# Block means of the values: from accumulating loads to twelve matmuls, with a new order of work

## The chip, the cores and the metric

The kernel runs on one core of a Trainium2 chip. The metric is the device time of one execution in microseconds (us); lower is better. Besides it there is a profile of one execution, taken by the hardware profiler.

## What is computed

Local and global attention over 2 batches, 8 heads, 768 positions of 64 values, followed by two feed-forward layers over the 1536 tokens of 512 values. The values' block means are what the change is about: `v_sum`, the mean over each block of 32 positions, 24 blocks per batch.

```python
k_sum = k.reshape(B, H, nb, 32, D).max(axis=3)
v_sum = v.reshape(B, H, nb, 32, D).mean(axis=3)
scores_l = scale * q @ k^T, kept where |i - j| < 16, else -1e9
scores_s = scale * q @ k_sum^T + log(32)
a = softmax(concat(scores_l, scores_s))
x = a @ concat(v, v_sum)                    # (1536, 512)
h = x @ w_in;  x = (h * sigmoid(1.702 h)) @ w_out
h = x @ w_in2; x = (h * cos(h)) @ w_out2
```

## The kernel before

**Tiling.** The attention goes by units of 128 queries, of which there are 12 (6 per batch). A unit scores its queries against a window of 96 keys per half unit and the 24 block maxima of its batch, so each row of scores has 120 columns; it then transposes the probabilities on TensorE and multiplies them with a values tile whose first 96 rows are the window and whose last 24 rows are the block means. The feed-forward layers go by three token tiles of 512 (four units each), and in each by 16 pieces of 128 hidden values: `h` matmuls (L697), the activation on ScalarE and VectorE, `out` matmuls (L793) that add into four PSUM banks. Weights and activations are each split into a high and a low part, and three products of them are added.

**The start.** The first four units ("early") are worked in two halves of four heads each, so there are eight groups of early scores ("early s", L406), of masking on VectorE (L413), of exponentials on ScalarE (L420), of transposes ("early t", L455), of copies out of PSUM (L465) and of value products ("early pv", L435). Their values tiles are `vw` and the three `vy`. The first weights (`raw` tiles, 1 MB each, L604) are loaded and split beside this (L616 scaling on ScalarE, L622 and L626 on VectorE, then L643 high part and L647 low part). Units 4 to 11 ("main") are put between the matmuls of the first layer's token tiles and use PSUM banks `a0` and `a1` for scores (L406), transposes (L521) and products.

**The block means before.** The rows of a batch's values are loaded so that several rows of one block come to the same partition: a first load writes a tile (L312, SP's queue), and further loads, issued by GpSimd, add to it during the transfer (`accum_op=ALU.add`, L317). Batch 0 has three tiles of 128 partitions with one accumulating load each. Batch 1 has one tile of 96 partitions with seven accumulating loads, each of which waits for the one before. A matmul with a constant selection matrix `blk` (L380, `vsum_mm`) adds what is left over partitions and scales: three matmuls for batch 0 in an "h" bank (`vsum0`), one for batch 1 in bank `a0` (`vsum1`, created at step 2 of the feed-forward loop, L961). ScalarE and GpSimd copy batch 0's means into the values tiles (`put_vsum`, L352); ScalarE copies batch 1's into `vsb` (L963), from where they go into `vw` before unit 6.

**The order of work.** Nothing is ordered by the place in the source alone. Every step is an `Op` with an engine, an estimated duration and what it depends on; `Ring` objects add the dependences of reused buffers. `order_of` (L177) runs a list scheduler over the steps with a priority per kind (the path length to the end plus `BONUS`), models TensorE's two clock levels with `PE_COLUMNS`, and the steps are then emitted in the order of their planned starts. Each engine takes its instructions in that order. The chain `wanted` (L926) fixes the order of SP's first loads: keys of the first half, queries, mask, identity, `blk`, the three tiles of batch 0's values, keys and queries of the second half, the window values of unit 0, the first weights, the other window values, the second weights. Batch 1's values and keys come behind that (L935).

Of the kernel before, what the change touches and what calls it, by code (L numbers as in the profile page):

```python
# [10 lines left out]
FP32 = mybir.dt.float32  # L11
# [3 lines left out]
ALU = mybir.AluOpType  # L15
# [4 lines left out]
DM, DFF = 512, 2048  # L20
# [32 lines left out]
PE_COLUMNS = {"s": 1920, "early s": 960, "t": 960, "pv": 1800, "early pv": 900, "vsum": 1920, "vsum1": 1440}  # L53
PE_DEFAULT = 3 * U
BONUS = {
    "add vf": -3414.5, "add vf1": -18784.9, "added vf": -13944.7, "added vf1": 6958.2, "at": 11219.4,
    "early at": 4634.7, "early exp": -16393.5, "early load v": -13487.3, "early load w": 3402.3,
    "early norm": -7393.4, "early pv": -21291.9, "early s": -1812.0, "early sum": -5913.0, "early t": 11259.2,
    "early ttr": -13278.6, "early w hi": -9898.3, "early w join": 1295.3, "early w lo": -17457.0,
    "early w low": 8007.6, "early w scale": -8113.8, "early xc": -3323.6, "early xl": -3755.5, "evac": 13034.7,  # L60
    "exp": 3944.6, "g hi": -14757.5, "g lo": -32277.0, "gate": 6833.5, "h": 1746.4, "ksum": -9033.2,
    "load blk": -15626.5, "load ident": -10094.2, "load k": 32.4, "load k1": -5996.2, "load kf0": 11676.2,
    "load kf1": -9957.5, "load mask": 17224.8, "load q": 5269.3, "load qf0": -25960.1, "load qf1": 9488.3,
    "load v": 509.5, "load vf": 17019.9, "load vf1": -16213.9, "load w": -6084.3, "norm": 18693.0, "out": 1747.8,
    "put ksum": 7597.4, "put vsum": -13657.5, "put vsum pool": 517.6, "pv": -5659.2, "s": -293.9, "store": -8775.6,
    "sum": -7343.5, "t": 22163.2, "ttr": -7908.6, "vsb": 368.0, "vsum": 4596.7, "vsum1": -11612.0, "w hi": -3717.9,
    "w join": -5696.0, "w lo": 4131.9, "w low": 4594.6, "w scale": -6735.7, "x hi": -18171.4, "x lo": -12909.2,
    "xc": -5390.2,
# [142 lines left out]
def local_global_attention_two_ffn(  # L211
# [56 lines left out]
    vf = [[w_p.tile([n, DM], FP32, name="vf", tag="w1") for _ in range(a)] for n, a in ((128, 3), (GW, 1))]  # L268
# [8 lines left out]
    blk = ex[1][:, 1536:1792]  # L277
    ksum = ex[1][:, 1792:1984].rearrange("p (b h n) -> p b h n", b=B, h=H // 2)
# [28 lines left out]
    s_vf = [[], []]  # L307
    for b in range(B):
        n = (2, 8)[b]
        r = v[b].rearrange("(t p r) d -> t p r d", p=vf[b][0].shape[0], r=n)  # L310
        for a, t in enumerate(vf[b]):
            o = ring["w1"].take(dma(("load vf", "load vf1")[b], (0.9, 0.7)[b], t, r[a, :, 0, :]), True)  # L312
            d_vf[b].append(o)
            for k in range(1, n):
                go = op(
                    ("add vf", "add vf1")[b], "POOL", 1.1,
                    lambda t=t, i=r[a, :, k, :]: nc.gpsimd.dma_start(out=t, in_=i, accum_op=ALU.add), o  # L317
                )
                o = op(("added vf", "added vf1")[b], "DMA", (0.9, 0.7)[b], lambda: None, go)
                for x in (go, o):  # L320
                    ring["w1"].use(x)
            s_vf[b].append(o)
# [50 lines left out]
    def vsum_mm(b, tag, parts):  # L373
        ps, mm = {}, None
        for a, (sel, t, n, dep) in enumerate(parts):
# [10 lines left out]
            ring["w1"].use_of(n, dep)  # L386
# [3 lines left out]
    def vsum0(tag):  # L390
        return vsum_mm(0, tag, [(blk[:, 16 - 8 * a:16 - 8 * a + GC], vf[0][a], a, s_vf[0][a]) for a in range(3)])

    def vsum1(tag):
        return vsum_mm(1, tag, [(blk[0:GW, 136:136 + GC], vf[1][0], 3, s_vf[1][0])])
# [457 lines left out]
    for a in range(1, UT):  # L852
        ring["w1"].use_of(3 + a, d_v[a])
# [197 lines left out]
```

## Time and profile before

| | |
|---|---|
| median of 3 runs | 600.13 us (599.36 to 601.23) |
| the profiled execution | 600.15 us, of which 598.4 us are its span |
| TensorE (PE) busy | 582.9 us, 97% |
| its weight loads (PEld) | 473.7 us, 79% |
| VectorE (DVE) busy | 396.5 us, 66% |
| ScalarE (ACT) busy | 294.4 us, 49% |
| GpSimd (POOL) busy | 13.1 us, 2% |
| mean granted clock of TensorE | 0.981 |
| DMA | 55.07 MB; plain queue 52.36 MB, accumulating queue 2.16 MB |

The span is what lies between the first and the last instruction. An engine's busy time is an average over stages that have different limits, so the table says only which engine can be the bound as a whole; where it waits, and for whom, is read from the views of single stretches below. A matmul in 32-bit floats leaves two records, so "x2" of the block means (L380) is one matmul. Records of successive matmuls overlap: what one costs in a row of them is read from the distance of starts. A row of the view by stretch holds the stretch, its length, the busy time (and number of instructions) of PE, PEld, DVE, ACT and POOL in this order, the granted clock of TensorE as a share of 2.4 GHz, the busy share of the DMA engines and what they moved in GB/s.

### The profile page before, as it was taken

The numbers are of one execution on the slowest core, as the hardware profiler recorded it, in microseconds if no ns is written. First come the engines' busy times: TensorE is split into PE (matmuls) and PEld (weight loads), VectorE is DVE, ScalarE is ACT, GpSimd is POOL, SyncE is SP. The second block draws the span as 40 slices with busy tenths as digits, with TensorE's granted clock in tenths as the row PEclk, the third lists the DMA queues.
The fourth block names the chain that finished last, engine by engine and source line by source line (L and its number), as shares of the span: only waits on it lengthen the run. The fifth ranks groups of instructions, "written<-read, shape, count | busy, mean of one in ns | idle before, by whom it ended". The sixth has DMA issues, their size and how long they took to land.

```text
span 598.4 us, 8609 instructions
## 1 busy us (share of the span) xinstructions
PE 582.9 (97%) x3310; PEld 473.7 (79%) x3310; DVE 396.5 (66%) x810; ACT 294.4 (49%) x607; POOL 13.1 (2%) x21
## 2 busy tenths in 40 slices
PE   6999998999999999999999999999999999999996
PEld 4578886888888888888888888888888888888885
DVE  5789897856322244778779866667666667765663
ACT  4788666856212454756657633234433344433332
POOL 2011110000000000000000000000000000000000
PEclk8699998999999999999999999999999999999999
DMA  8969897652000130545550000000100000100001
GB/s 297 300 223 292 262 268 231 200 154 72 1 0 1 44 97 28 212 146 206 211 174 38 1 1 0 1 1 0 72 0 2 0 1 0 71 1 1 0 1 71
DMA packets 24281, 55.07 MB, mean 92 GB/s; under 512 B 9904, under 2 KB 14384, under 8 KB 20144
## 3 DMA queue, kind: packets, MB, share of 16 engines
q1 hardware_dynamic: 23024, 52.36, 26.1%
q0 software_dynamic: 1216, 2.16, 2.2%
q8 instruction: 26, 0.43, 0.3%
q14 instruction: 15, 0.12, 0.1%
HBM read 51.37 MB, written 3.15 MB: 91 GB/s over the span
## 4 chain that ended last, share of the span: by engine, by line
PE 88%; DMA 7%; ACT 2%; DVE 1%; issue 1%; SPq 0%; POOL 0%; ACTq 0%
PE h_ps L697 41%; PE acc L793 41%; DMA vf<-in_v_dram 4%; DMA raw<-in_w_dram 4%; PE x_ps L435 2%; PE s_ps L406 1%; PE t_ps L521 1%; DVE wc L626 1%; ACT wc L616 1%; PE vs_ps L380 1%; SPq L261 0%; DVE w L647 0%; PE t_ps L455 0%; ACT ex L420 0%; DVE raw L622 0%
## 5 line engine op out<-in xcount | busy, mean ns | idle before, releaser
L697 PE MATMUL h_ps<-xh,w 128*128 128x512 f32 x1152 | 302.8, 392 | 0.0
L793 PE MATMUL acc<-g,w 128*128 128x512 f32 x1152 | 300.9, 390 | 0.0
L697 PEld LDWEIGHTS h_ps<-xh,w 128*128 128x128 f32 x1152 | 215.4, 188 | 46.3 <-issue 1.7
L793 PEld LDWEIGHTS acc<-g,w 128*128 128x128 f32 x1152 | 215.7, 188 | 45.4 <-issue 0.6
L753 ACT CAST g<-gt 128x512 fp32r<-128x512 f32 x96 | 59.7, 622 | 138.3 <-PE acc L793 132.2
L757 DVE TENSOR_TENSOR g<-gt,g 128x512 fp32r<-128x512 f32 x96 | 66.1, 689 | 88.3 <-ACT g L753 88.1
L745 ACT ACTIVATE gt<-gt,half_pi 128x512 f32<-128x512 f32 x48 | 34.7, 723 | 64.2 <-DVE gt L741 64.0
L749 DVE TENSOR_TENSOR gt<-gt,h_ps 128x512 f32<-128x512 f32 x48 | 33.0, 688 | 25.5 <-ACT gt L745 25.5
L647 DVE TENSOR_TENSOR w<-wc,w 128x512 fp32r<-128x512 f32 x64 | 43.5, 686 | 1.0 <-ACT w L643 0.7
L721 ACT ACTIVATE gt<-h_ps 128x512 f32<-128x512 f32 x48 | 28.6, 597 | 30.2 <-PE h_ps L697 28.6
L643 ACT CAST w<-wc 128x512 fp32r<-128x512 f32 x64 | 38.5, 617 | 7.9 <-DVE wc L626 7.9
L626 DVE SCALAR_TENSOR_TENSOR wc<-wc,raw 128x1024 uint32<-128x1024 uint32 x32 | 39.2, 1224 | 3.1 <-ACT wc L616 1.9
L616 ACT ACTIVATE wc<-raw 128x1024 f32<-128x1024 f32 x32 | 37.0, 1156 | 7.3 <-DMA raw<-in_w_dram 7.2
L729 DVE TENSOR_SCALAR gt<-gt 128x512 f32<-128x512 f32 x48 | 20.5, 427 | 24.6 <-ACT gt L721 24.2
L725 DVE SCALAR_TENSOR_TENSOR gt<-gt,h_ps 128x512 f32<-128x512 f32 x48 | 32.8, 683 | 3.4 <-ACT gt L719 3.0
L733 DVE SCALAR_TENSOR_TENSOR r<-gt,h_ps 128x512 f32<-128x512 f32 x48 | 33.4, 696 | 1.6
L737 DVE SCALAR_TENSOR_TENSOR gt<-gt,r 128x512 f32<-128x512 f32 x48 | 32.9, 686 | 1.4
L719 ACT ACTIVATE gt<-h_ps 128x512 f32<-128x512 f32 x48 | 28.4, 592 | 6.5 <-PE h_ps L697 4.7
L622 DVE TENSOR_SCALAR raw<-raw 128x1024 uint32<-128x1024 uint32 x32 | 22.1, 690 | 3.8 <-DMA raw<-in_w_dram 3.8
L741 DVE TENSOR_SCALAR gt<-gt 128x512 f32<-128x512 f32 x48 | 20.4, 424 | 0.9
L420 ACT ACTIVATE ex<-ex 128x120 f32<-128x120 f32 x32 | 12.2, 394 | 6.8 <-DVE ex L413 6.8
L672 DVE TENSOR_TENSOR xh<-xf,xh 128x512 fp32r<-128x512 f32 x20 | 12.8, 685 | 3.7 <-ACT xh L669 3.7
(73 smaller groups left out, 276.8 us busy)
## 6 DMA issues: line engine op xcount, KB each, us to landing
raw<-in_w_dram SPq DMA_DIRECT2D x32, 1024.0 KB, 5.3
win<-in_vwin_dram SPq DMA_DIRECT2D x9, 384.0 KB, 3.5
win<-in_kT_dram SPq DMA_DIRECT2D x16, 192.0 KB, 4.1
out_dram<-xf SPq DMA_DIRECT2D x12, 256.0 KB, 2.1
win<-in_qT_dram SPq DMA_DIRECT2D x8, 256.0 KB, 3.9
kf<-in_kT_dram SPq DMA_DIRECT2D x4, 400.0 KB, 4.3
k<-in_kT_dram SPq DMA_DIRECT2D x4, 400.0 KB, 7.9
vf<-in_v_dram POOLq DMA_DIRECT2D x7, 192.0 KB, 5.9
```

What stands on the lines that cost most here:

```text
L616: nc.scalar.activation(out=t.bitcast(FP32), in_=raws[m][:, :, 1].bitcast(FP32), func=ACTF.Prelu, scale=REBIAS, alpha=SIGN)
L626: nc.vector.scalar_tensor_tensor(out=t, in0=t, scalar=3, in1=raws[m][:, :, 0], op0=ALU.logical_shift_left, op1=ALU.bitwise_or)
L643: nc.scalar.copy(out=w[:, 0, :], in_=mids[m][:, 512 * a:512 * (a + 1)].bitcast(FP32))
L647: nc.vector.tensor_tensor(out=w[:, 1, :], in0=mids[m][:, 512 * a:512 * (a + 1)].bitcast(FP32), in1=w[:, 0, :].bitcast(FP32), op=ALU.subtract,)
L697: nc.tensor.matmul(out=hs[i], lhsT=w[:, a, c], rhs=x[:, b, :], start=(k == 0 and n == 0), stop=(k == KD - 1 and n == 2),)
L733: nc.vector.scalar_tensor_tensor(out=r, in0=gts[i], scalar=-C1, in1=hs[i], op0=ALU.mult, op1=ALU.add)
L737: nc.vector.scalar_tensor_tensor(out=gt, in0=gt, scalar=-C2, in1=rs[0], op0=ALU.mult, op1=ALU.add)
L745: nc.scalar.activation(out=gt, in_=gt, func=ACTF.Sin, bias=half_pi)
L749: nc.vector.tensor_tensor(out=gt, in0=gt, in1=hs[i], op=ALU.mult)
L753: nc.scalar.copy(out=g[:, 0, :], in_=gts[i])
L757: nc.vector.tensor_tensor(out=g[:, 1, :], in0=gts[i], in1=g[:, 0, :].bitcast(FP32), op=ALU.subtract)
L793: nc.tensor.matmul(out=accs[d][:, 0:U], lhsT=w[:, a, 128 * d:128 * (d + 1)], rhs=g[:, b, :], start=(f == 0 and n == 0), stop=(f == NF - 1 ...
```

## The change

The accumulating loads are gone. Each batch's 768 rows of values are loaded plainly by SP into three tiles of 128 partitions with two rows of 512 values each (`vf`, 128 x 2 x 512), six loads of 512 KB. Each batch's means are six matmuls over 128 rows each, twelve in all, that add in one PSUM bank. `vsum(1, "a0")` and the copy to `vsb` are created ahead of the feed-forward loop in place of its step 2. In SP's first loads only the first tile of batch 0's values stands ahead of the second half of the keys; the other two follow the second half of the queries; all three tiles of batch 1's values stand between the window values and the second weights. The constant `blk` has 140 columns in place of 256. `vf` takes six buffers of the ring of second weights in place of four, so the numbers of the buffers behind it move by two. The priorities (`BONUS`) that steer the planner are new throughout, and with them the order of work on every engine.

```diff
--- before.py
+++ after.py
@@ -50,22 +50,21 @@
 PE_TICK = 10.24 / 3
 PE_BUSY = 3060
 PE_FILL = {0: 2460.0, 1: 3168.0}
-PE_COLUMNS = {"s": 1920, "early s": 960, "t": 960, "pv": 1800, "early pv": 900, "vsum": 1920, "vsum1": 1440}
+PE_COLUMNS = {"s": 1920, "early s": 960, "t": 960, "pv": 1800, "early pv": 900, "vsum": 1920, "vsum1": 1920}
 PE_DEFAULT = 3 * U
 BONUS = {
...
 }
 PUT_VSUM = ("ACT", "POOL", "POOL")
 SHARED = {
@@ -265,7 +264,7 @@
     nc.scalar.activation(out=warm, in_=warm, func=ACTF.Exp)
     kf = [w_p.tile([128, SP], FP32, name="kf", tag="w0") for _ in range(H // 2)]
     qf = [w_p.tile([128, 2, U], FP32, name="qf", tag="w0") for _ in range(2)]
-    vf = [[w_p.tile([n, DM], FP32, name="vf", tag="w1") for _ in range(a)] for n, a in ((128, 3), (GW, 1))]
+    vf = [[w_p.tile([128, 2, DM], FP32, name="vf", tag="w1") for _ in range(S // 256)] for _ in range(B)]
     vy = [w_p.tile([GC, 2, DM], FP32, name="vy", tag="w1") for _ in range(UT - 1)]
     sm_main, at_main = [w_p.tile([128, 1024], FP32, name=n, tag="w1") for n in ("sm_main", "at_main")]
     k1 = [w_p.tile([128, SP], FP32, name="k1", tag="w0") for _ in range(H // 2)]
@@ -274,8 +273,8 @@
     at_early = [x[:, 512 * j:512 * j + 512] for x in [g_p.tile([128, 1024], FP32, name="at_early", tag="g")
                                                       for _ in range(2)] for j in range(2)]
     vsb = ex[1][0:GC, 1024:1024 + DM]
-    blk = ex[1][:, 1536:1792]
-    ksum = ex[1][:, 1792:1984].rearrange("p (b h n) -> p b h n", b=B, h=H // 2)
+    blk = ex[1][:, 1536:1676]
+    ksum = ex[1][:, 1676:1868].rearrange("p (b h n) -> p b h n", b=B, h=H // 2)
     wz = wc_p.tile([128, 512], FP32, name="wz", tag="wc")
     nc.gpsimd.memset(wz, 0.0)
     wps = bank("h", "wps")
@@ -304,22 +303,10 @@
     d_mask = dma("load mask", 0.6, mask_sb, maskc)
 
     d_vf = [[], []]
-    s_vf = [[], []]
     for b in range(B):
-        n = (2, 8)[b]
-        r = v[b].rearrange("(t p r) d -> t p r d", p=vf[b][0].shape[0], r=n)
+        r = v[b].rearrange("(t a p) d -> t p a d", p=128, a=2)
         for a, t in enumerate(vf[b]):
-            o = ring["w1"].take(dma(("load vf", "load vf1")[b], (0.9, 0.7)[b], t, r[a, :, 0, :]), True)
-            d_vf[b].append(o)
-            for k in range(1, n):
-                go = op(
-                    ("add vf", "add vf1")[b], "POOL", 1.1,
-                    lambda t=t, i=r[a, :, k, :]: nc.gpsimd.dma_start(out=t, in_=i, accum_op=ALU.add), o
-                )
-                o = op(("added vf", "added vf1")[b], "DMA", (0.9, 0.7)[b], lambda: None, go)
-                for x in (go, o):
-                    ring["w1"].use(x)
-            s_vf[b].append(o)
+            d_vf[b].append(ring["w1"].take(dma(("load vf", "load vf1")[b], 1.4, t, r[a]), True))
     for _ in range(UT + 1):
         ring["w1"].take(boot(), True)
     d_blk = dma("load blk", 0.37, blk, blkc)
@@ -383,15 +370,13 @@
 
             mm = op(("vsum", "vsum1")[b], "PE", 0.86, fn, dep, d_blk, mm)
             ring[tag].take(mm) if a == 0 else ring[tag].use(mm)
-            ring["w1"].use_of(n, dep)
             ring["w1"].use_of(n, mm)
         return (lambda: ps[0]), mm
 
-    def vsum0(tag):
-        return vsum_mm(0, tag, [(blk[:, 16 - 8 * a:16 - 8 * a + GC], vf[0][a], a, s_vf[0][a]) for a in range(3)])
-
-    def vsum1(tag):
-        return vsum_mm(1, tag, [(blk[0:GW, 136:136 + GC], vf[1][0], 3, s_vf[1][0])])
+    def vsum(b, tag):
+        n = S // 128
+        return vsum_mm(b, tag, [(blk[:, 20 - 4 * a:20 - 4 * a + GC], vf[b][a // 2][:, a % 2, :], 3 * b + a // 2,
+                                 d_vf[b][a // 2]) for a in range(n)])
 
 
     def edge(i):
@@ -835,7 +820,7 @@
     for hp in range(4):
         ring["w0"].use_of(hp, ks[hp])
     pk = [put_ksum(0, hf, ks[2 * hf], ks[2 * hf + 1]) for hf in range(2)]
-    vs0, vm0 = vsum0("h")
+    vs0, vm0 = vsum(0, "h")
     vput = [ring["h"].use(put_vsum("ACT", vs0, vw, vm0))]
     for a, eng in enumerate(PUT_VSUM):
         o = put_vsum(eng, vs0, vy[a], vput[0] if eng == "POOL" else vm0)
@@ -843,14 +828,14 @@
             ring["rawC"].use_of(0, o)
         else:
             ring["h"].use(o)
-        ring["w1"].use_of(4 + a, o)
+        ring["w1"].use_of(6 + a, o)
         vput.append(o)
     w_load(0)
     w_load(1)
     sm_ring, at_ring = Ring(6), Ring(4)
     d_v = [load_v(i, vt[i]) for i in range(UT)]
     for a in range(1, UT):
-        ring["w1"].use_of(3 + a, d_v[a])
+        ring["w1"].use_of(5 + a, d_v[a])
     v_last, acs = [], []
     for n in range(2 * UT):
         hf, i = divmod(n, UT)
@@ -873,7 +858,7 @@
         hf, i = divmod(n, UT)
         pv = early_values(n, i, hf, acs[n], vt[i], [d_v[i], vput[i]], at_ring)
         if i:
-            ring["w1"].use_of(3 + i, pv)
+            ring["w1"].use_of(5 + i, pv)
         else:
             v_last.append(pv)
     first_done = pv
@@ -901,7 +886,7 @@
             space = lambda k: (sm_main, at_main)[k]
 
             def extra(x):
-                for n in (3 + UT, 4 + UT):
+                for n in (5 + UT, 6 + UT):
                     ring["w1"].use_of(n, x)
 
         begin = [*need["k"], need["q"]] + ([(first_done,)] if i == UT else [])
@@ -923,16 +908,18 @@
                 ring["xf1"].use_of(0, x)
 
 
-    wanted = [d_kf[0], d_kf[1], d_qf[0], d_mask, d_id, d_blk, *d_vf[0], d_kf[2], d_kf[3], d_qf[1], d_v[0], w_loads[0],
-              *d_v[1:], w_loads[1]]
+    wanted = [d_kf[0], d_kf[1], d_qf[0], d_mask, d_id, d_blk, d_vf[0][0], d_kf[2], d_kf[3], d_qf[1], *d_vf[0][1:],
+              d_v[0], w_loads[0], *d_v[1:], *d_vf[1], w_loads[1]]
     for x, y in zip(wanted, wanted[1:]):
         y.deps.append((x,))
     need = {"k": [load_k(UT), *pk], "q": load_q(UT), "v": [load_v(UT, vw, *v_last), vput[0]]}
     main_rings, late_rings = (Ring(1), Ring(1)), (Ring(1), Ring(1))
-    vs1_done = [None]
+    vs1, vm1 = vsum(1, "a0")
+    vs1_done = [ring["a0"].use(op("vsb", "ACT", 0.5, lambda: nc.scalar.copy(out=vsb, in_=vs1()[0:GC]), vm1))]
+    ring["xf1"].use_of(0, vs1_done[0])
     for x in (*need["k"], need["q"], *need["v"]):
         ring["rawC"].use_of(0, x)
-    for x in (need["k"][0], need["q"], *d_vf[1], *d_k1):
+    for x in (need["k"][0], need["q"], *d_k1):
         x.deps.append((wanted[-1],))
     for x in (vm0, *pk):
         ring["xf1"].use_of(0, x)
@@ -958,10 +945,6 @@
                     w_load(m + 1)
             elif m >= NF and m + 3 < 2 * NF:
                 w_load(m + 3)
-        if i == 2:
-            vs1, vm1 = vsum1("a0")
-            vs1_done[0] = ring["a0"].use(op("vsb", "ACT", 0.5, lambda: nc.scalar.copy(out=vsb, in_=vs1()[0:GC]), vm1))
-            ring["xf1"].use_of(0, vs1_done[0])
         if i == NF * (NTU - 1) - 2:
             for m in range(3):
                 w_load(NF + m)
@@ -1001,9 +984,8 @@
             rows = slice(64 * g, 64 * g + 64)
             mask[m, rows, 0:GW] = np.where(ok, 0.0, -8.0e9)[rows]
             mask[m, rows, GW:] = 8.0 * np.log(float(BLK))
-    blk = np.zeros((128, 256), np.float32)
-    blk[p, 16 + GW + 2 * p // BLK] = 1.0 / BLK
-    blk[p[:GW], 136 + GW + 8 * p[:GW] // BLK] = 1.0 / BLK
+    blk = np.zeros((128, 140), np.float32)
+    blk[p, 20 + GW + p // BLK] = 1.0 / BLK
     return np.ascontiguousarray(mask.transpose(1, 0, 2)), np.eye(128, dtype=np.float32), blk
```

## Rows read from the trace of the kernel before

**Rows 1.** Page, parts 1 and 2: TensorE, its share and busy tenths.

```profile
PE 582.9 (97%) x3310; PEld 473.7 (79%) x3310; DVE 396.5 (66%) x810; ACT 294.4 (49%) x607; POOL 13.1 (2%) x21
...
PE   6999998999999999999999999999999999999996
```

**Rows 2.** By stretch, start: busy us (count) per engine, clock, DMA share, GB/s.

```profile
7.92:12.00 4.08, 3.77 (x128) 3.66 (x128) 2.80 (x27) 2.97 (x16) 2.18 (x3) 0.68 1.04 389
16.00:20.00 4.00, 4.00 (x71) 3.24 (x70) 2.74 (x15) 2.53 (x11) 0.27 (x1) 0.50 1.03 311
22.00:25.80 3.80, 3.80 (x8) 1.07 (x4) 3.66 (x15) 3.80 (x18) 0.00 (x0) 0.50 1.11 266
27.00:30.00 3.00, 2.98 (x54) 1.88 (x54) 0.99 (x9) 1.91 (x2) 0.77 (x1) 1.00 1.02 388
```

**Rows 3.** By stretch around 93 us, the same columns.

```profile
92.50:94.83 2.33, 0.01 (x1) 0.01 (x1) 1.20 (x2) 1.66 (x2) 0.00 (x0) 0.98 1.01 376
94.83:96.00 1.17, 1.17 (x3) 0.64 (x3) 0.72 (x1) 0.41 (x1) 0.00 (x0) 0.50 0.24 63
```

**Rows 4.** Chain that ended last, at the start: start us, length us, what.

```profile
11.12 15.77 DMA vf<-in_v_dram
...
37.81 1.13 PE x_ps L435 x32
38.94 2.96 PE h_ps L697 x12
```

**Rows 5.** TensorE timeline, first 70 us: start, length, what [idle before].

```profile
7.92 0.56 PE L406 MATMUL s_ps<-kf,qf 64*64 64x96 f32 x16 [1.67 <-DMA qf<-in_qT_dram]
...
22.03 3.77 PE L380 MATMUL vs_ps<-vf,ex 128*120 128x512 f32 x4
26.93 1.12 PE L380 MATMUL vs_ps<-vf,ex 128*120 128x512 f32 x2 [1.13 <-DMA vf<-in_v_dram]
27.98 0.56 PE L406 MATMUL s_ps<-kf,qf 64*64 64x96 f32 x16
...
28.67 0.65 PE L455 MATMUL t_ps<-ident,ex 128*120 128x128 f32 x4
29.25 0.73 PE L435 MATMUL x_ps<-at_early,win 120*64 120x64 f32 x16
...
47.06 2.88 PE L793 MATMUL acc<-g,w 128*128 128x512 f32 x12
```

**Rows 6.** Chain that ended last, around 97 us.

```profile
96.88 1.28 PE h_ps L697 x3
...
98.91 0.68 PE h_ps L697 x3
```

**Rows 7.** Waits of TensorE: who for whom, us in total, times, longest.

```profile
PE t_ps L455 <- ACT at_early L465: 1.7, 2, 1.1
...
PE t_ps L455 <- ACT ex L420: 1.4, 1, 1.4
```

**Rows 8.** Timeline of all engines around 93 us.

```profile
93.11 1.18 ACT L616 ACTIVATE wc<-raw 128x1024 f32<-128x1024 f32 x1 [2.78 <-DMA raw<-in_w_dram]
...
94.83 2.06 PE L380 MATMUL vs_ps<-vf,ex 96*120 96x512 f32 x2 [2.33 <-ACT xf L556]
```

**Rows 9.** DMA queues from 40 to 95 us: packets, MB, share of 16 engines.

```profile
q0 software_dynamic: 784, 1.38, 15.9%
```

**Rows 10.** DMA queues in the first 40 us, the same columns.

```profile
q1 hardware_dynamic: 4608, 9.77, 74.6%
q0 software_dynamic: 432, 0.79, 10.7%
```

**Rows 11.** Weight load issued at 11.85 us: KB, us to landing.

```profile
raw<-in_w_dram SPq DMA_DIRECT2D x1, 1024.0 KB, 18.6
```

**Rows 12.** Timeline of SP's queue: the issue of the second weight load.

```profile
11.85 0.35 SPq L604 DMA_DIRECT2D raw<-in_w_dram  x1
```

**Rows 13.** Timeline of all engines: the second weights' scaling.

```profile
35.49 1.21 ACT L616 ACTIVATE wc<-raw 128x1024 f32<-128x1024 f32 x1
```

More of the change, by code (lines that the diff above doesn't have):

```diff
@@ L52 @@
 PE_FILL = {0: 2460.0, 1: 3168.0}
-PE_COLUMNS = {"s": 1920, "early s": 960, "t": 960, "pv": 1800, "early pv": 900, "vsum": 1920, "vsum1": 1440}
+PE_COLUMNS = {"s": 1920, "early s": 960, "t": 960, "pv": 1800, "early pv": 900, "vsum": 1920, "vsum1": 1920}
 PE_DEFAULT = 3 * U
 BONUS = {
[L56 to L68, printed above, removed]
@@ new lines @@
+    "at": 11606.9, "early at": 10830.3, "early exp": -7221.5, "early load v": 2883.4, "early load w": -15614.8,
+    "early norm": -10661.2, "early pv": -12137.5, "early s": 2587.2, "early sum": -14725.7, "early t": 30824.5,
+    "early ttr": -13905.0, "early w hi": -27229.4, "early w join": 12696.8, "early w lo": -16203.3,
+    "early w low": 1565.8, "early w scale": -925.5, "early xc": -756.0, "early xl": -12802.5, "evac": 6059.9,
+    "exp": 1220.5, "g hi": -3927.8, "g lo": -13901.3, "gate": 27267.5, "h": -1998.7, "ksum": -6206.9,
@@ new lines @@
+    "load blk": -6683.0, "load ident": -10704.3, "load k": 836.3, "load k1": -4.1, "load kf0": 2191.3,
+    "load kf1": 3812.2, "load mask": 30501.6, "load q": -8888.0, "load qf0": -2966.3, "load qf1": -4206.6,
+    "load v": -15224.9, "load vf": 9391.4, "load vf1": -7121.6, "load w": 3455.7, "norm": 5088.1, "out": -1997.3,
+    "put ksum": 17391.6, "put vsum": -13264.9, "put vsum pool": -7968.7, "pv": -2004.8, "s": -15323.3,
+    "store": -3428.7, "sum": -29034.1, "t": 11882.7, "ttr": -4823.5, "vsb": 7119.1, "vsum": 10953.0,
@@ L69 @@
+    "vsum1": 2305.1, "w hi": -6152.9, "w join": -13918.2, "w lo": 752.4, "w low": 1549.1, "w scale": 2849.4,
+    "x hi": -7791.2, "x lo": -4217.1, "xc": -12444.7,
 }
```

## The prediction

> **What bounds the kernel now.** I read the engine shares of the page first. TensorE is busy for 97% of the span [rows 1], so only two things can move the end: the work that TensorE has, and the stretches in which it waits or runs at the lower clock. The second view, the table by stretch, finds those stretches: at the start [rows 2] and around 93 us [rows 3]. In the slices between them, and from there to the end, TensorE is full [rows 1].
>
> *The start* runs from 7.92 us, when the first queries are there, to 38.94 us, when the last early value product is done [rows 4, 5]: 31.0 us. I price what TensorE does in it at full clock from starts that follow each other: a group of early scores 0.69 us (27.98 to 28.67), a group of transposes 0.58 (28.67 to 29.25) [rows 5], a group of value products 0.57 (1.13 for two) [rows 4]. There are eight of each: 14.7 us. One 128x512 matmul of the block means takes 3.77 / 2 = 1.88 us at half clock, so 0.94 at full clock; the one at 26.93 took 1.05 with its pipeline still empty [rows 2, 5]. Three make 2.8 us. Six matmuls of the first layer, which are done by then, add 1.4 (0.68 for three, [rows 6]). That is 18.9 us of work in 31.0 us: **12.1 us are lost**. Of these 4.2 are waits: 1.1 for the accumulating loads [rows 5], 1.7 and 1.4 of the transposes for ScalarE [rows 7]. The other 7.9 are mostly the clock, which stands at 0.50, the 1.2 GHz level, in the stretches up to 25.8 us and at 1.00, the 2.4 GHz level, from 27 us on [rows 2]. The chain of waits goes through the accumulating loads there: 15.77 us in one piece, up to 26.89 [rows 4].
>
> *Around 93 us* TensorE stands still for 2.33 us, and the clock is then at 0.50 [rows 3]. The instruction that waits is the block mean of the second batch, for its PSUM bank a0. ScalarE has to empty that bank, and stands just then behind a weight load that landed late [rows 8]: the copy out of the bank is queued behind the weight scaling (L616), which had waited 2.78 us for its data. The matmul then takes 2.06 us, and the next three of the first layer 1.28 in place of 0.68 [rows 6, 8].
>
> **Part 1, the block mean of batch 1 leaves the middle of the stream.** This gives back 2.33 of waiting, 2.06 of matmul and 0.60 of slow clock: **5.0 us**. At the least only the 2.06 comes back, if the late weight load stops TensorE anyway (a rival below). I take the whole, because the seven accumulating loads of batch 1 leave the stretch too: their queue took 15.9% of the 16 DMA engines over 55 us, 8.7 us of all the DMA there is, in a stretch that is full of weight loads [rows 9]. What is late next there would again be the weight load, with up to 8.7 us less in front of it.
>
> **Part 2, nine more matmuls at the start.** Twelve in place of three (the fourth of before was counted in part 1). Nine times 0.94 is **8.5 us** at full clock. The bounds are 9.5 (at 1.05) and 17 (all at half clock, 1.88) [rows 5]. No other engine can hide them; only TensorE's own lost time can.
>
> **Part 3, what of the 12.1 us is filled or saved.** The wait of 1.1 for the accumulation goes, since nothing accumulates. The first tile of values is now ahead of the second half of the keys in SP's queue, so that two of the means can be calculated at about 12 us, in the hole before the first transposes. They are dense 512-column work. At 22.03 two such matmuls at half clock were followed by full clock [rows 2, 5]; the same two ten microseconds earlier should bring the full clock near 17 us. I count what is then still lost:
> - up to 12 us as now: 4.08 us of time for four groups of scores of 0.69, so 1.3 [rows 2];
> - from 12 to 17 us two means and a group of transposes at half clock: 2 x 0.94 + 0.58 = 2.5 of work that takes twice that, so 2.5;
> - waits that stay: some 0.7 of the 1.7 of the transposes for ScalarE (an estimate; the bounds are 0 and 1.7, [rows 7]).
>
> Together 4.5 in place of 12.1, so 7.6 comes back against 8.5 of new work: the start ends **0.9 us later**. Bounds: 3.6 us earlier if nothing is lost, 7.4 us later if all but the 1.1 stays lost.
>
> A row that speaks against it: from 16 to 20 us TensorE was busy for 4.00 of 4.00 us with scores and transposes, and the clock stayed at 0.50 [rows 2]. [...] The Trainium skill (TensorE: Matmul & The Clock Gate, Part 4: PE-mode transpose) goes further and says that a transpose does not count as busy for the clock gate in the way that a matmul does. By that rule, with transposes planned between the first means, the time would be that of the first rival; the row agrees with the rule, but scores ran among the transposes and it can't tell them apart.
>
> **Part 4, the loads.** The first batch's values are loaded once, plainly, in place of a load and an accumulation. In the first 40 us the accumulating queue moved 0.79 MB in 10.7% of 40 us = 4.3 us of all engines; the plain queue moved 9.77 MB in 29.8 us, so that 0.79 MB cost 2.4 there [rows 10]: 1.9 us are saved. Against this the 1.57 MB of the second batch now go ahead of the second weight load: 1.57 / 9.77 x 29.8 = 4.8 us. That load landed at 11.85 + 18.6 = 30.5 [rows 11, 12] and would land near 33.4; without the saving and at the 266 GB/s of the slowest stretch [rows 2] it would be 36.4. It was first used at 35.49 [rows 13], and the first product that needs its second half began at 47.06 [rows 5]. I cost it at nothing; the cover is gone when it lands past about 38. On SP two more issues stand ahead of it, each under half a microsecond like the one in [rows 12]. GpSimd loses ten issues, off every path. The copy of batch 1's mean (one ScalarE instruction) moves from 97 us into the start; what is queued behind it there is the chain of copies and exponentials, and bank a0 is held until it is done, for which the first main scores wait. I bound it at 0 to 0.6 and take 0, TensorE being the bound by then.
>
> **Part 5, the new order.** Prices for the planner change; TensorE's queue behind 100 us has no gap to close [rows 1], so a new order can only keep or lose there. Taken at 0; the bound is one more stall like the one at 93 us, 2.33 + 0.60 = 2.9.
>
> **The sum.** The profiled execution took 600.15 us, of which 598.4 are its span, and the median is 600.13; the two stand for one another. 600.15 - 5.0 + 0.9 = **596.0 us**. A measurement of this kernel tells about 0.3%, 1.8 us, from no change.
>
> **The rivals.**
> - *The clock rises late.* The first two means do not lift it, because transposes stand between them or the load lands late, and it is half until 22 us. Then 12 to 22 us loses 5.0 in place of 2.5, the start loses 7.0, and 8.5 - 5.1 - 5.0 = -1.6: 598.5. For it: the row of 16 to 20 us. Against it: the means are dense and there are six for the first batch.
> - *The stall at 93 us stays.* The weight load is what was late, and TensorE only met it at this instruction. Then 0.9 - 2.1 = -1.2: 599.0. For it: ScalarE's wait of 2.78 for that load [rows 8]. Against it: the DMA time that comes free.
> - *Slower: the means wait in TensorE's queue as they did before.* TensorE takes its instructions in order; a mean that stands ahead of transposes and value products while its load is under way holds these up, as at 26.93, and the clock stays down because TensorE waits. The new matmuls then fill no hole. Lost at the start stays 11.0, and 8.5 - 1.1 - 5.0 = +2.4: 602.6. It decides from a loss of 8.6 us on (12.1 - 8.5 + 5.0); past 10.4 the kernel is measurably slower. For it: six loads are now awaited, the last three behind nearly all others. Against it: the new loads depend on nothing, where the accumulations each waited for the load before.
> - *Better: the clock holds from 12 us.* Only 1.3 + 0.7 = 2.0 is lost: 8.5 - 10.1 - 5.0 = -6.6: 593.5.
>
> **How the numbers follow.** Forecast 0.42, clock late 0.15, stall stays 0.10, slower 0.18, better 0.15. Faster by over 0.3% are the forecast and the better case, 0.57; within 0.3% are the late clock and the stall, 0.25; slower 0.18. The range goes from 592.0, the better case with 1.5 less of the waits, to 603.0, the slower case; about 0.1 is left out at each end. The likeliest case alone holds 594.0 to 598.0.
>
> **What would show it.** Right: no TensorE wait near 93 us and a clock of 1.00 there; full clock by 17 to 18 us; the last early value product, with all twelve means and six first-layer matmuls done, near 39.8 us. Wrong: a TensorE wait of over 1 us on a load of values; half clock beyond 20 us; a stall of weights between 40 and 100 us; ScalarE's scaling of the second weight load begun after 39 us; any new TensorE gap behind 100 us.

## The result: 594.0 us, and the profile after

The changed kernel took 594.04 us (median of 4 runs, 593.55 to 596.12) against 599.98 us before in the same comparison: a ratio of 0.9881 with a 95% interval from 0.9843 to 0.9919. Measured again beside the last experiments it took 593.63 us, a ratio of 0.9885 (0.9860 to 0.9909). The profiled execution took 593.72 us, 591.9 of them its span; the one of before had 600.15 and 598.4.

The page of the changed kernel, with TensorE's share, the clock in 40 slices, and the chain of work that ended last:

```profile
PE 581.7 (98%) x3326; PEld 471.9 (80%) x3326; DVE 395.8 (67%) x810; ACT 294.0 (50%) x607; POOL 5.2 (1%) x11
...
PE   7799999999999999999999999999999999999997
...
PEclk9999999999999999999999999999999999999999
...
PE 95%; DMA 4%; SPq 1%; DVE 0%; issue 0%
```

TensorE is busy for 1.2 us less than before [rows 1] although it has eight matmuls more, the full clock (9) stands in every slice, and the chain is TensorE for 95%. The table by stretch (columns as in [rows 2]):

```profile
7.92:12.00 4.08, 3.78 (x118) 2.78 (x109) 3.76 (x28) 3.50 (x19) 0.00 (x0) 1.00 1.04 406
...
16.00:20.00 4.00, 4.00 (x16) 2.00 (x14) 3.19 (x17) 3.23 (x16) 0.00 (x0) 1.00 1.00 303
...
22.00:25.80 3.80, 1.70 (x36) 1.52 (x36) 3.10 (x15) 3.13 (x11) 2.01 (x2) 1.00 1.02 241
...
92.50:95.00 2.50, 2.50 (x40) 1.90 (x39) 2.50 (x6) 1.99 (x4) 1.51 (x2) 1.00 0.88 351
```

Against [rows 2] the clock is 1.00 where it was 0.68 and 0.50. Against [rows 3] TensorE is busy throughout 92.5 to 95 us. But from 22 to 25.8 us it is busy for 1.70 of 3.80 us only: the lost time is still there, of another kind. TensorE's timeline and its waits in the same stretch:

```profile
7.39 0.56 PE L391 MATMUL s_ps<-kf,qf 64*64 64x96 f32 x16 [1.02 <-DMA qf<-in_qT_dram]
...
9.89 1.12 PE L367 MATMUL vs_ps<-vf,ex 128*120 128x512 f32 x2
...
24.80 0.70 PE L420 MATMUL x_ps<-at_early,vy 120*64 120x64 f32 x16 [2.10 <-ACT ex L405]
...
26.44 0.70 PE L420 MATMUL x_ps<-at_early,vy 120*64 120x64 f32 x16 [0.35 <-DMA vy<-in_vwin_dram]
...
29.10 4.45 PE L367 MATMUL vs_ps<-vf,ex 128*120 128x512 f32 x10
...
37.23 5.78 PE L682 MATMUL h_ps<-xh,w 128*128 128x512 f32 x24
```

```profile
PE x_ps L420 <- DMA vy<-in_vwin_dram: 0.6, 2, 0.3
```

The first mean stands at 9.89 us between two groups of early scores. The wait of 2.10 before 24.80 is named after ScalarE, but the exponentials that ScalarE worked on then belong to later transposes. The first value product of a `vy` tile also needs that tile, and the DMA view has its load, issued at 9.53 us:

```profile
vy<-in_vwin_dram SPq DMA_DIRECT2D x1, 384.0 KB, 15.1
```

9.53 + 15.1 = 24.6: the product waited for the window load, and so did the two after it (0.35, 0.25). In the chain that ended last, the start is no longer held by the accumulation [rows 4] but by the third `vy` load, up to 27.84 us; the five means are in it too:

```profile
11.51 16.33 DMA vy<-in_vwin_dram
...
29.26 4.29 PE vs_ps L367 x10
```

**Where the 6.5 us between the two profiled executions came from.** The first layer could begin at 37.30 us, against 38.94 less the two groups of its matmuls that were done by then (1.4), so 37.6: 0.3 us. From there to TensorE's end 555.5 us became 550.4: 5.1 us. From the end of the last copy to the end of the span 4.57 us became 3.47: 1.1 us, for which I have no cause. These are the two copies (before, then the changed kernel):

```profile
593.14 0.69 DVE L818 COPY xf<-acc 128x512 f32<-128x512 f32 x1 [0.67 <-PE acc L793]
```

```profile
587.74 0.69 DVE L803 COPY xf<-acc 128x512 f32<-128x512 f32 x1 [0.67 <-PE acc L778]
```

### The profile page after: what moved, and what is told of

Its sections match the earlier page's. It is cut to its first block, busy times and chain, and to the rows that moved or that the text cites. A ratio compares the mean times of both kernels' runs of the same rounds, so it can differ in the third digit from the quotient of the medians.

```text
span 591.9 us, 8625 instructions
## 1 busy us (share of the span) xinstructions
PE 581.7 (98%) x3326; PEld 471.9 (80%) x3326; DVE 395.8 (67%) x810; ACT 294.0 (50%) x607; POOL 5.2 (1%) x11
## 4 chain that ended last, share of the span: by engine, by line
PE 95%; DMA 4%; SPq 1%; DVE 0%; issue 0%
PE acc L778 45%; PE h_ps L682 44%; DMA vy<-in_vwin_dram 3%; PE x_ps L420 2%; PE s_ps L391 1%; PE t_ps L506 1%; DMA kf<-in_kT_dram 1%; PE vs_ps L367 1%; SPq L260 1%; PE t_ps L440 0%; DVE xf L803 0%
## 5 line engine op out<-in xcount | busy, mean ns | idle before, releaser
L714 DVE TENSOR_SCALAR gt<-gt 128x512 f32<-128x512 f32 x48 | 20.5, 427 | 25.0 <-ACT gt L706 24.6
L718 DVE SCALAR_TENSOR_TENSOR r<-gt,h_ps 128x512 f32<-128x512 f32 x48 | 33.4, 696 | 1.6
L405 ACT ACTIVATE ex<-ex 128x120 f32<-128x120 f32 x32 | 12.2, 386 | 6.7 <-DVE ex L398 6.7
L405 ACT ACTIVATE room<-room 128x120 f32<-128x120 f32 x32 | 12.2, 383 | 5.6 <-DVE room L398 5.6
```

The source lines that it names most:

```text
L718: nc.vector.scalar_tensor_tensor(out=r, in0=gts[i], scalar=-C1, in1=hs[i], op0=ALU.mult, op1=ALU.add)
```

## The experiments

Ratios are against the kernel before, measured on the same chip, with 95% intervals. "Start" is where the first layer's matmuls take over for good: the run of 12 that began at 38.87 us in the kernel before, the run of 24 that began at 37.23 in the changed one. It also moves with the landing of the first queries (7.92 us and 7.39 there), which differs from one execution to the next, so I give that time where it matters. Each run has one profile, and its clock and waits are those of one execution. Several runs leave work out, so that the means they calculate are incomplete; they are for timing only.

**Only the priorities exchanged.** In `after_oldprio` the changed kernel gets the old `BONUS`, in `before_newprio` the kernel before gets the new one; the planner orders both.

```diff
-BONUS = { ...new... }
+BONUS = { ...old... }
```

> The changed kernel with the priorities (BONUS) of the kernel before; the planner makes its own order from them. Theory A (the gain is the change itself: no accumulation, means early, no stall at 93 us): 592 to 597 us, no TensorE wait of over 1 us between 40 and 580 us. Theory B (the gain is the new order): 599 us or more, with a stall of weights or means somewhere behind 40 us.

> The kernel before with the priorities of the changed kernel (the kinds that have none there get zero). Theory A: 599 to 603 us, the late mean of batch 1 still makes TensorE wait for over 1 us near 93 us and the clock still falls to 0.50 from 10 to 26 us. Theory B: 597 us or less.

Measured: 0.9957 (0.9939 to 0.9975) for the first, 1.0100 (1.0060 to 1.0139) for the second. Table by stretch and TensorE's timeline of `after_oldprio`, then TensorE's waits in `before_newprio`:

```profile
12.00:16.00 4.00, 4.00 (x36) 1.70 (x34) 3.73 (x12) 1.98 (x11) 0.63 (x1) 0.51 1.07 353
...
30.00:33.00 3.00, 2.54 (x33) 2.20 (x34) 1.43 (x4) 1.14 (x4) 0.00 (x0) 0.50 1.05 414
```

```profile
30.46 1.01 PE L441 MATMUL t_ps<-ident,ex 128*120 128x128 f32 x4 [2.66 <-ACT ex L406]
...
43.03 1.05 PE L392 MATMUL s_ps<-win 64*64 64x120 f32 x32
```

```profile
PE vs_ps L379 <- DMA vf<-in_v_dram: 10.0, 4, 6.5
```

With the old priorities the same matmuls end the start at 43.03 us (there main scores come first, then the first layer), 5.8 us later than in the changed kernel, 0.8 of them because the first queries were there at 8.22 us: the clock is at half twice, and TensorE waits 2.66 us for exponentials that stand late on ScalarE. This profiled execution took 601.68 us where the median of ten is 599.40, so it overstates the loss. With the new priorities the old loads make TensorE wait for 10.0 us, 6.5 of them at one mean and 2.4 at batch 1's mean near 96 us. So neither theory holds alone: the change without its order is worth 0.4%, the order without the change costs 1.0%, together they give 1.2%.

**Do the first two means hold the clock?** Same order as the changed kernel, two instructions not issued:

```diff
-                if a == 0:
+                if b == 0 and a < 2:
+                    return
+                if a == (2 if b == 0 else 0):
                     ps[0] = bank(tag, "vs_ps")
...
```

> The changed kernel in its own order, but the first two of the twelve matmuls (the ones at 9.89 and 11.63 us) are left out, so batch 0's means lack eight blocks. Theory A (these two hold the clock): the clock falls to 0.50 between 10 and 16 us, the last early value product ends 1 to 3 us later than 37.2 us, and the time is 595 to 597 us although 1.9 us of work are gone. Rival C (the clock would hold anyway, through the earlier queries or by chance): clock 1.00 throughout, and 592 to 594 us.

Measured: 0.9908 (0.9887 to 0.9929).

```profile
12.00:16.00 4.00, 2.46 (x39) 2.00 (x36) 3.93 (x17) 3.12 (x17) 0.63 (x1) 0.50 1.08 353
16.00:20.00 4.00, 4.00 (x37) 2.35 (x37) 3.90 (x24) 2.22 (x11) 0.00 (x0) 0.50 1.01 288
```

```profile
38.76 5.74 PE L684 MATMUL h_ps<-xh,w 128*128 128x512 f32 x24
```

The clock is at 0.50 from 12 to 20 us and the start ends 1.5 us later (0.6 of it because the first queries were there at 7.95), with 1.7 us less to do. The time did not fall. Theory A's signs came, at their lower end: these two matmuls pay for themselves. But "hold" is the wrong word. In this profile the clock fell at 9.8 us, among the third group of scores and so ahead of the place of the first mean, and stayed at half for about 10.2 us. In the five profiles with these two means in the same places (the changed kernel twice and three runs below) it fell ahead of the first mean too, or not at all: before 21 us it was at half for 0, 3.4, 3.4, 7.0 and 0 us. So with the two means the half clock is shorter; why it falls in one execution and not in another is open. The mean clocks of all executions agree: 0.991 to 0.997 in the four without the two means, 0.993 to 0.999 in eight of the changed kernel (averages 0.993 and 0.997).

**Is the clock enough for the kernel before?** Two dense matmuls in the same two places:

```diff
+        seen = 0
         for o in order_of(ops):
             o.fn()
+            if o.kind == "early s":
+                seen += 1
+                if seen in (3, 4):
+                    nc.tensor.matmul(out=wps, lhsT=kf[0][:, 0:128], rhs=kf[0][:, 128:640], start=True, stop=True)
```

> The kernel before with two added 512-column matmuls on loaded keys, whose result nobody reads, behind the third and fourth group of early scores, where the changed kernel has its first two means. Theory A: the clock stays at 1.00 from 10 to 26 us, but the start still waits for the accumulating loads until about 27 us, so the last early value product ends near 38 us and the time is 598 to 600 us: the clock alone is worth under 2 us here. Rival D (the clock is the whole gain of the start): the last early value product ends by 35 us and the time is 596 us or less.

Measured: 0.9987 (0.9961 to 1.0013), no difference.

```profile
7.92:12.00 4.08, 3.78 (x107) 2.70 (x102) 3.31 (x29) 3.61 (x19) 2.77 (x3) 1.00 1.03 388
12.00:16.00 4.00, 2.33 (x35) 1.32 (x36) 3.90 (x15) 3.17 (x16) 0.32 (x2) 1.00 1.08 307
16.00:20.00 4.00, 3.51 (x67) 2.71 (x56) 3.26 (x20) 2.54 (x10) 0.00 (x0) 0.61 1.06 313
```

```profile
PE vs_ps L380 <- DMA vf<-in_v_dram: 3.4, 2, 2.3
```

The clock was 1.00 up to 16 us, not up to 26 as theory A had it, and TensorE then waited 3.4 us in place of 1.1 [rows 5] for the accumulating loads. The start ended 0.3 us sooner (38.53), but the first queries were there 0.6 us sooner (7.28): the start itself is no shorter. What the clock gains goes into the two added matmuls and the next wait, so theory A is right that the start waits for the accumulating loads, and rival D is out.

**Batch 0 without its accumulations, alone and with the two dense matmuls.**

```diff
-                    lambda t=t, i=r[a, :, k, :]: nc.gpsimd.dma_start(out=t, in_=i, accum_op=ALU.add), o
+                    (lambda: None) if b == 0 else (lambda ...the same...), o
```

> The kernel before in its own order, with the three accumulating loads of batch 0 left out (its means then hold half of their rows). Theory A (two things hold the start back, the accumulating loads and the half clock): the wait of 1.1 us at 26.9 us goes and the three means end earlier, but the clock is still 0.50 up to about 22 us; the time falls by 1 to 2.5 us. Rival D (the clock alone matters): under 0.5 us.

> The kernel before with both edits: the two added 512-column matmuls behind the third and fourth group of early scores, and batch 0's accumulating loads left out. Theory A: only now does the clock pay; it is 1.00 through most of 10 to 26 us, the last early value product ends 3 to 5 us before 38.9 us, and the time falls by 3 to 5 us, more than the two edits alone together. Rival G (ScalarE or the window loads hold the start by then): the time falls by under 2.5 us.

Measured: 0.9959 (0.9933 to 0.9986) alone, 0.9975 (0.9956 to 0.9994) with both. TensorE's timeline with both edits, and its waits:

```profile
35.98 3.03 PE L697 MATMUL h_ps<-xh,w 128*128 128x512 f32 x12
```

```profile
PE x_ps L435 <- ACT win L359: 3.2, 1, 3.2
PE vs_ps L380 <- ACT xf L556: 1.7, 1, 1.7
...
PE h_ps L697 <- DVE gt L725: 1.2, 1, 1.2
```

Alone, the edit gave 2.5 us, within theory A; but its ten times fall into two groups, 595.2 to 596.8 us (four) and 598.5 to 601.8 (six), and its profile (601.54) is of the second, so I do not compare its start. With both edits the start ends at 35.98 us, 2.9 us before that of the kernel before, 1.0 of it because the first queries were there at 6.90. Theory A had 3 to 5 us in the start and as much at the end; about 1.5 us reach the end, which is rival G's size. Rival G's reason is there too: with the clock and the loads out of the way, TensorE waits 3.2 us for ScalarE's copy of the means (L359), which stands behind a weight scaling and eight exponentials. Behind the start there is a wait of 1.2 us for an activation near 85 us, and the stall at batch 1's mean is still there with 1.7. Both edits together gave no more than the one. A gain in the start need not reach the end as long as such waits stand behind it; how much each took is not shown.

**Why are the weights late?** Batch 1's accumulating loads left out (as above, with `b == 1`):

> The kernel before in its own order, with the seven accumulating loads of batch 1 left out (its means then hold an eighth of their rows). Theory A (the stall at 93 us comes from the DMA time of these loads: the weight load that ScalarE waits for is late): the wait of TensorE before batch 1's mean is under 0.5 us, the clock stays near 1.00 there, and the time falls by 2.5 to 4 us. Rival E (the order is at fault: the mean asks for bank a0 before it can be free): the wait stays over 1.5 us and the time falls by under 1.5 us.

Measured: 0.9944 (0.9925 to 0.9962), 3.4 us. The stretch around 93 us, then ScalarE's wait for weights from 57 to 95 us in this kernel and in the kernel before:

```profile
92.50:94.83 2.33, 2.33 (x16) 1.68 (x12) 1.64 (x3) 1.59 (x3) 0.00 (x0) 1.00 0.90 306
```

```profile
ACT wc L616 <- DMA raw<-in_w_dram: 0.7, 2, 0.5
```

```profile
ACT wc L616 <- DMA raw<-in_w_dram: 6.7, 4, 3.0
```

TensorE no longer stands still at 93 us (2.33 of 2.33 us busy, against 0.01 [rows 3]), though the order is untouched, and ScalarE waits 0.7 us for weights where it waited 6.7. Theory A holds: the stall came from these loads, and the order was not at fault. The run takes away the bytes of the loads together with their accumulation, so it does not show which of the two makes the weights late.

**And with the instruction gone, but the loads kept?**

```diff
-mm = op(("vsum", "vsum1")[b], "PE", 0.86, fn, dep, d_blk, mm)
+mm = op(("vsum", "vsum1")[b], "PE", 0.86, (lambda: None) if b else fn, dep, d_blk, mm)
...
```

ScalarE's copy behind it (`vsb`) stays, and copies a constant of the mask in place of the mean.

> The kernel before in its own order, with batch 1's mean matmul left out (its means are then a constant); the accumulating loads stay. Theory A (TensorE stood still only for this instruction): no TensorE wait of over 0.5 us near 93 us, and the time falls by 4 to 5.5 us. Rival F (the late weight load stops TensorE at the next instruction anyway): a wait of 1 to 2.5 us near 93 us stays, at matmuls of the first layers, and the time falls by 1 to 2.5 us.

Measured: 1.0027 (1.0004 to 1.0051), nothing gained. ScalarE's wait, and TensorE's timeline behind 100 us:

```profile
ACT wc L616 <- DMA raw<-in_w_dram: 7.3, 5, 2.8
```

```profile
108.78 1.93 PE L521 MATMUL t_ps<-ident,sm_main 128*120 128x128 f32 x8 [3.88 <-DVE sm_main L429]
```

The stall at 93 us is gone and comes back 16 us later with 3.88 us, at transposes that wait for VectorE, on which two joins of weights (L626, 1.23 us each) stand ahead of the attention step. TensorE was ready for them at 104.9 us, 3.3 us sooner than in the kernel before (108.16), but VectorE's result came no sooner. Theory A is out. Rival F was right in its point, but neither in the place nor in the size (it had a gain of 1 to 2.5 us): while the loads are slow, taking the instruction away gains nothing. With the loads left out, in the run before, this wait is not there.

**What do the added matmuls cost?** Five of batch 1's six left out of the changed kernel:

```diff
-                if a == 0:
+                if b == 1 and a < 5:
+                    return
+                if a == (5 if b == 1 else 0):
                     ps[0] = bank(tag, "vs_ps")
...
```

> The changed kernel unaltered, beside the three edits of it: 593 to 597 us, as its own times say, 0.985 to 0.992 of the kernel before.

> The changed kernel in its own order, with five of batch 1's six mean matmuls left out (batch 1's means lack 20 of 24 blocks). Theory A (they are paid in full, since TensorE is the bound from 29 us on): 4 to 4.5 us less than the changed kernel, five times 0.86. Rival H (they stand in time that TensorE would lose anyway, to ScalarE and the window loads): under 1.5 us less.

Measured: 0.9870 (0.9844 to 0.9896) against 0.9885 (0.9860 to 0.9909) for the changed kernel: 0.9 us, where full payment would give 4.3 and a ratio near 0.981. Table by stretch and start, then the same of the changed kernel in that comparison:

```profile
25.80:27.00 1.20, 1.05 (x19) 1.01 (x20) 0.82 (x4) 0.44 (x3) 0.00 (x0) 0.93 1.00 283
27.00:30.00 3.00, 2.58 (x23) 1.77 (x21) 1.10 (x2) 1.63 (x2) 0.00 (x0) 0.50 1.08 390
30.00:33.00 3.00, 3.00 (x36) 2.52 (x36) 1.28 (x5) 2.81 (x12) 0.00 (x0) 0.50 1.03 413
```

```profile
25.95 0.71 PE L422 MATMUL x_ps<-at_early,vy 120*64 120x64 f32 x16 [2.17 <-ACT ex L407]
...
36.53 5.74 PE L684 MATMUL h_ps<-xh,w 128*128 128x512 f32 x24
```

```profile
7.39:12.00 4.61, 4.18 (x98) 3.71 (x98) 2.78 (x25) 2.83 (x15) 0.00 (x0) 0.63 1.03 400
...
27.00:30.00 3.00, 2.79 (x24) 1.67 (x21) 2.08 (x5) 3.00 (x13) 0.00 (x0) 1.00 1.08 407
```

```profile
36.30 5.76 PE L682 MATMUL h_ps<-xh,w 128*128 128x512 f32 x24
```

Without the five matmuls the clock falls to 0.50 behind the wait before 25.95 us, stays there for 6.8 us, and the start ends where it ended with them. Rival H's size came out: they are nearly free. Its reason, waits that they fill, seems the smaller part. The mean clock was 0.990 to 0.994 in the four executions without them, 0.993 to 0.999 in the eight of the changed kernel. The averages, 0.992 and 0.997, differ by 0.005 of 592 us, so an estimate of 3.0 us of TensorE's work goes to the clock, if TensorE was busy while the clock was low; that is most of the 3.4 us by which the 4.3 failed to pay. The five do not prevent the fall: it came at 26.8 us, ahead of their place (28.2 and 29.1 in the changed kernel's profiles), and in `after_w0_vy1` below it came behind a like wait with the five in place and lasted 3.4 us:

```profile
27.00:30.00 3.00, 2.92 (x25) 2.45 (x25) 1.28 (x3) 2.43 (x11) 0.00 (x0) 0.60 1.06 399
```

That they bring the clock back sooner fits these profiles; it is not shown by itself. The changed kernel's own second profile also shows that its clock is not safe: here it fell between 8 and 12 us (0.63) and the start still ended 0.9 us sooner than in the first.

**A step on: the window loads ahead of the first weights.** The changed kernel's order, with one issue moved on SP:

```diff
+        held, seen = None, 0
         for o in order_of(ops):
+            if o is w_loads[0]:
+                held = o
+                continue
             o.fn()
+            if o in d_v[1:]:
+                seen += 1
+                if seen == 3:
+                    held.fn()
```

The second run has `seen == 1`.

> The changed kernel with one step moved: the first weight load is issued behind the three window loads (vy) in SP's queue in place of ahead of them; every other engine keeps its order. Theory I (the value products wait for the window loads: 24.6 us landing, 2.1 + 0.6 us of TensorE): these land about 3 us sooner, the waits go, and the time falls by 1 to 2.5 us against the changed kernel. Rival J (the first weights are then late: ScalarE scales them at 26.7 us, and stands still until they land): the wait moves to ScalarE and the time is within 1 us of the changed kernel or above it.

> As the run before, but the first weight load is issued behind the first window load only. Theory I: the wait of 2.1 us falls to about 1 us, the weights land about 1 us later, which nobody feels, and the time falls by 0.5 to 1.2 us against the changed kernel. Rival J: no difference of over 0.5 us.

Measured: 0.9898 (0.9876 to 0.9921) and 0.9899 (0.9872 to 0.9925), no better than the changed kernel. The first one's waits, a stretch and its start, then the second one's wait:

```profile
PE t_ps L440 <- ACT at_early L450: 1.1, 2, 0.9
```

```profile
12.00:16.00 4.00, 4.00 (x40) 1.68 (x44) 3.97 (x20) 3.11 (x17) 0.63 (x1) 0.66 1.10 337
```

```profile
38.07 5.74 PE L682 MATMUL h_ps<-xh,w 128*128 128x512 f32 x24
```

```profile
PE x_ps L420 <- DMA vy<-in_vwin_dram: 2.2, 1, 2.2
```

With all three window loads ahead, no product waits for them and ScalarE does not wait for weights, so theory I's mechanism is there; but in the profiled execution the clock was down till about 15 us and the start ended at 38.07. With one load ahead the wait moves to the next load (2.2 us), the clock falls behind it, and the start ended at 38.39. Whether the first would gain at full clock is open. No complete version that was tried beats the changed kernel.

## Why the prediction was right, and where its steps were not

**The total.** 596.0 was forecast with a range of 592.0 to 603.0; 594.0 was measured, and 593.7 in the profiled execution. The sign and the two places were right. Of the 2.3 us by which the profiled execution was missed, 1.1 lie in the start and 1.1 behind the last copy, which the prediction did not consider and whose cause is open. That the total came so close is in part luck, as part 3 shows. One of the prediction's own signs of being wrong did come: a TensorE wait of over 1 us for a load of values, the 2.10 for a window load.

**Part 1, batch 1's mean out of the stream.** Forecast 5.0, measured 5.1 between the start and TensorE's end. The reason given, that the accumulating loads make the weights late, is shown: without these loads the stall is gone in the old order (3.4 us), with them it comes back when the instruction is removed. That it is their accumulating, more than their bytes, rests on [rows 9] and [rows 10] and on no run. ScalarE's wait for weights from 57 to 95 us fell from 6.7 to 0.4 us in the changed kernel. The rival "the stall stays" had the mechanism of what happens when only the matmul is taken away, though there not even its 2.1 us came back.

**Part 2, nine matmuls for 8.5 us.** Mis-sized. A mean took 4.29 / 5 = 0.86 us in a row of five, not 0.94, so nine are 7.7. And the claim that only TensorE's lost time can hide them was right, but the sum treated that time as a fixed store to draw on. Leaving out five of them gained 0.9 in place of 4.3 us, and the mean clock was lower without them: the work changes how much time is lost.

**Part 3, the lost time.** Its total was right (4.5 forecast; 29.9 us from 7.39 to 37.30 less 14.7 and 12 x 0.86 of work leaves 4.9), by two errors that cancel. The clock: forecast at half until 17 us, 3.8 us lost up to there; in the profiled execution it never fell. That was the better rival. The first mean stood at 9.89 us ahead of the fourth group of scores, not at 12 us behind it, but that alone does not explain it: in the changed kernel's second profile the clock fell at about 8.2 us, ahead of any mean, and was back at about 11.6. So whether the forecast or the better rival came was in part chance of the execution. The first rival did not come; from 16 to 20 us four means and two transposes ran at 1.00. The Trainium skill's rule that had spoken for it (TensorE: Matmul & The Clock Gate, Part 4: PE-mode transpose) is neither shown nor refuted by that, since the means stood among the transposes. The waits: forecast 0.7, measured 3.7 (2.10, 0.35 and 0.25 for window loads, and three others of 0.30 to 0.36). The step that failed is "waits that stay": I took them from the transposes' wait for ScalarE [rows 7] and did not ask when the `vy` loads land. They are hardly later than before, where the three took

```profile
vy<-in_vwin_dram SPq DMA_DIRECT2D x3, 384.0 KB, 15.6
```

and the first landed at 9.75 + 13.7 = 23.5 us. There the first product of a `vy` tile began at 30.06 us, and the wait was hidden; the changed kernel was ready for it at 22.7. The better rival's 593.5 came out, but not by its sum. The start's 1.1 us add up so: the first queries landed 0.5 us sooner (7.39 against 7.92), twelve means at 0.86 in place of 0.94 are 1.0 less, and 0.4 more was lost.

**Part 4, the loads.** The second weight load landed at 19.45 + 14.7 = 34.1 us (forecast 33.4), was scaled at 36.27 and stalled nobody, as costed:

```profile
raw<-in_w_dram SPq DMA_DIRECT2D x1, 1024.0 KB, 14.7
```

The landing is near the forecast by another way. Three more issues stand ahead of it on SP, not two, and SP waited between them, so the load went out 7.6 us later than before [rows 12] and then took 14.7 us in place of 18.6 [rows 11]:

```profile
12.88 5.25 SPq L260 DMA_DIRECT2D vf<-in_v_dram  x3
...
19.45 0.35 SPq L589 DMA_DIRECT2D raw<-in_w_dram  x1
```

**Part 5, the new order at nothing.** Wrong for the start. With the old priorities the changed kernel keeps 2.6 of its 6.9 us: the order decides whether the means stand where TensorE has time for them. Behind 100 us the argument held, TensorE has no gap there.

**The slower rival** (means that hold up TensorE's queue) did not come, because the plain loads of batch 0 land early: its six means were done by 19.6 us. Its mechanism is real all the same: it is what the new priorities do to the old loads, 7.6 us of waits in the start.

## What to carry to other kernels

The bill for a transfer can come at a place that does not use it: here accumulating loads, which took more DMA time for their bytes than the plain ones [rows 10], made weight loads late that shared the DMA engines with them. Removing the instruction at which an engine waits can be worth nothing when the cause is upstream; take the load away first and see whether the wait follows. Work added to the bound engine in a start full of waits may be nearly free, and here the mean clock was higher with it, but only where the order puts it into the holes. Once one wait is filled, look up when each other input lands: a load that is no later than before can become the next wait.

## What was not expected of the hardware

- The clock at the start differs between executions of one program. The changed kernel ran with mean clocks of 0.999 and 0.993 and spans of 591.9 and 594.3 us; in its second profile the clock fell among the first scores, in the first it did not. Behind the same two dense matmuls it fell to half between 16 and 20 us in `before_dense2` (0.61) and held there (1.00) with batch 0's accumulations left out.
- Small matmuls did not lift the clock from 16 to 20 us in the kernel before [rows 2], but in `before_no_acc0` it fell at 8.8 us and was back at 1.00 from 12.2 us on, with no matmuls between but early scores. So that row is no rule:

```profile
7.92:12.00 4.08, 4.04 (x128) 4.04 (x128) 2.85 (x26) 2.93 (x15) 0.00 (x0) 0.60 1.04 402
12.00:16.00 4.00, 1.44 (x11) 0.87 (x8) 3.97 (x16) 3.49 (x18) 0.00 (x0) 0.93 1.09 292
```

- The first scores, which wait for the first queries, began between 6.9 and 8.2 us in the fourteen profiles, with the same loads ahead of them.
- From the last copy to the end it is 4.3 to 4.6 us in the six programs with the order of before and 3.5 to 3.7 in the other eight, with the same four stores. It is 1.1 of the 6.5 us of the change, and the cause is open.
